# A four-layer forward and backward pass: the order of the weight-gradient products, the layout of dq, and which tiles are turned by DMA

## The chip, the cores and the metric

The kernel runs on one core of one Trainium2 chip. The metric is the device time of one execution in microseconds, the median of three runs. Engines: PE (TensorE, matrix products and 128x128 transposes), DVE (VectorE), ACT (ScalarE), POOL (GpSimd), and SP (SyncE), which here issues the DMA transfers, in the order of its own queue. PSUM, which PE writes, has eight banks.

## The reference

The forward pass runs four residual layers over x of 2048 x 640: linear attention (A), sliding-window attention (B), A, B, with one set of weights for both A and one for both B. 32 heads of 20 columns; the window of B is 256 tokens.

```python
def _A_ref(x, wqkv, wo):
    q, k, v = split(x @ wqkv)
    pq, pk = phi(q), phi(k)          # phi: t + 1 above 0, exp(t) below, + 1e-6
    kv, z = einsum("bhsd,bhse->bhde", pk, v), einsum("bhsd->bhd", pk)
    o = einsum("bhqd,bhde->bhqe", pq, kv) / (einsum("bhqd,bhd->bhq", pq, z)[..., None] + 1e-6)
    return merge(o) @ wo

def _B_ref(x, wqkv, wo):
    q, k, v = split(x @ wqkv)
    p = softmax(where(mask, q @ k.T * Dh ** -0.5, -1e9))   # 0 <= i - j < 256
    return merge(p @ v) @ wo

x = x + _A_ref(_layernorm(x), A_wqkv, A_wo)
x = x + _B_ref(_layernorm(x), B_wqkv, B_wo)
x = x + _A_ref(_layernorm(x), A_wqkv, A_wo)
x = x + _B_ref(_layernorm(x), B_wqkv, B_wo)
```

The outputs are the last x and the gradients of a given grad_out with respect to x and to the four weight matrices. Each weight gradient is a product over all tokens of two layers: for W, normed inputs (hn) transposed times the gradient of q, k, v (dq in DRAM, dqkv); for Wo, attention outputs (o) transposed times the layer's upstream gradient (gs).

## The kernel before

Tokens are cut into 16 tiles of 128, columns of 640 into five blocks of 128. The order of the instructions on each engine is written out by hand: each stage makes a list of (slot, function), sorts it, and runs it slot by slot. The table `PLACES` holds the slots. `put` queues a transfer for SP a few ticks later (delays in `PLACES["sp"]`), or issues it at once in the two linear stages, where SP's order is left to the framework. The stages of `passes`, in order of time:

- `forward`: layers 0 to 3. `plan_feat` makes the linear features of a tile; its `flip_h` turns hn2 into h2T on PE. `plan_front` of layer 2 needs the same turned tile again later to make the queries (`query`): it loads hn back from DRAM with a DMA transpose, as h3T. 
- `core` for layer 3, then for layer 1. A core walks over 8 chunks of two token tiles. Each chunk after the first has 24 visits, the first has 16, so that visits 24 to 47 are the second chunk (chunk 1). In `core_visit`, the visit that has just begun makes its scores s (PE), e = exp(s) (ACT) and the masks (POOL); the visit begun three steps earlier makes dp (PE) and ds = dp * e (DVE); ds is turned either on PE, with a copy out of PSUM by ACT or DVE (`flip_ds`, in which some extra warm transposes of the identity may stand), or by a DMA transpose, which `by_dma` says; the visit begun six steps earlier is multiplied into PSUM banks (`core_acc`). Every third visit `core_acc` adds the sums into the tile dq, [128, 2, 1920]: two token tiles by q, k and v columns. dp and s have one buffer each.
- `plan_behind` follows a core by about two chunks: dq is turned (`turn`), stored (`store`), multiplied by the turned weights WTB (`dh`), normalised backward (`ln`, `ln2`), multiplied by WoTA (`prod`) and summed into an outer product (`outer`). After the core its remainder, called left3 or left1, runs by itself.
- `plan_linear` does the backward pass of a linear layer, eight slots for each token tile: layer 2 between the two cores, layer 0 at the end.
- `weight_jobs` is a generator of all weight gradients. A job is one block of columns of one matrix (240 of W or 160 of Wo; twice that once `W.wide` is set). It keeps all rows of two layers in SBUF as lhs (2 x 16 tiles x 640) and the column block of 32 token tiles as rhs, and makes for each of the five row blocks m one PSUM sum over 32 products, copies it out (wr) and stores it. At m = 1 the next job's rhs is fetched, at m = 2, when the next job is of another matrix, its lhs. `W.lhs` lists the buffers that lhs take in turn; with `W.tight` the second lhs is fetched only after the job.
- `fill(us)` runs as many products of the generator as its credit of nominal time (columns / 2400 us for each product) allows. It is called in left1 with 0.7 us a slot from slot 25 on, in layer 0's stage with 0.8 us a slot, and with no bound afterwards. `W.tight` and `W.wide` change after layer 0's stage.

Before, the matrices come in the order B's Wo, B's W, A's Wo, A's W. `first` fetches the operands of the first job all at once at slot 3 of left1. PSUM during left1: two banks of the core's pool that are idle, four in a pool of its own, two for the weight jobs.

Of the kernel before, what the change touches and what calls it, by code (L numbers as in the profile page):

```python
# [11 lines left out]
ALU = mybir.AluOpType  # L12
# [3 lines left out]
P = 128  # L16
D = 640
# [31 lines left out]
    ld=[39.8, 61, 63, 69.7, 82.8],  # L49
    sp=[2.6, 1.1, -2.9, -3.4, 0.6, -3.8, 0.1, 0.4, 2, 1.8, 1.1, 0.8, 3, 1, 0.9, 0.5, 1.3, 1.1, 1, 1],  # L50
    ms=[1, -0.2, 20, 31.2, 39.5],
# [18 lines left out]
    xx=[1, 0, 1, 1, 0, 0, 0, 0, 1, 0, 1, 0, 0, 0, 0, 0, 0, 1, 0, 0, 1, 0, 0, 1],  # L70
    bd=[0, 1, 0, 0, 0, 0, 0, 1, 0, 1, 1, 0, 1, 1, 0, 0, 0, 1, 1, 1, 0, 1, 0, 0],
    sd=[0.7, 0, 0, 3, 3, 3, 3, 3.9, 0, 0, 3.2, 2.6, 3.3, 3.1],
    dj=[3, 21.9, 24, 3.5, 0.7, 8])

# [17 lines left out]
class Kern:  # L92
    def __init__(self, ctx, tc, x0, A_w, A_wo, B_w, B_wo, grad, outs):
        self.ctx, self.tc = ctx, tc
        self.nc = nc = tc.nc
        self.W = dict(A=A_w, B=B_w)
        self.Wo = dict(A=A_wo, B=B_wo)
        self.grad = grad
        self.out_x4, self.out_gx, dWA, dWoA, dWB, dWoB = outs
        self.dW = dict(A=dWA, B=dWB)  # L100
        self.dWo = dict(A=dWoA, B=dWoB)
        self.serial = 0
        self.queue, self.now, self.spm = [], 0, True
# [10 lines left out]
        self.x2 = d("x2", [T, D])  # L114
        self.WT = {k: d(f"WT{k}t", [P, NF * D]) for k in "AB"}
# [406 lines left out]
    def plan_front(self, st, la, lb, t, x, x_in, Wo, W, Wq=None):  # L522
# [6 lines left out]
        def load():  # L529
# [3 lines left out]
            else:  # L533
                x["h2T"] = st.fb.tile([P, DT, P], BF, name="h3T", bufs=2)
                self.dma(x["h2T"], self.rows(self.hn[la], t), transpose=True)

# [136 lines left out]
    def plan_feat(self, st, l, t, x, src, W):  # L673
# [5 lines left out]
        def flip_h():  # L679
            x["h2T"] = self.flip(st.ps, st.fl, x["hn2"], "h2T", P, DT, P, nc.scalar)  # L680

        def feat_(nm, c, split=False):
# [72 lines left out]
    @staticmethod  # L755
    def by_dma(n):

        return n >= 48 and PLACES["bd"][n % 24] == 1

# [91 lines left out]
    def core_acc(self, st, l, u):  # L851
# [28 lines left out]
        if u.last:  # L880
# [4 lines left out]

            def cols(tl, w, n):
                return tl[:, :, w * D:(w + n) * D].rearrange("p b (w q g x) -> p b w q g x", w=n, q=4, g=2)[:, :, :, u.qr, :, 40 * u.p:40 * u.p + 40]

            def acc(bk):
                return bk[:, 0:320].rearrange("p (b w g x) -> p b w g x", b=2, w=2, g=2)  # L890
            n = G * u.c + k
            if t0 + 2 < TT:
                nc.scalar.copy(st.part[:, n % (G + 1), :], st.acc[1][:, 0:320])
            else:
                for b in range(2):
                    nc.scalar.copy(cols(cur, 1, 2)[:, b], acc(st.acc[1])[:, b])  # L896
            if old is not None:
                for b in range(2):
                    nc.vector.tensor_tensor(out=cols(old, 1, 2)[:, b], in0=acc(st.acc[0])[:, b],
                                            in1=acc(st.part[:, (n + 1) % (G + 1), :])[:, b], op=ALU.add)  # L900
            nc.scalar.mul(cols(cur, 0, 1)[:, :, 0], st.acc[0][:, 320:480].rearrange("p (b g x) -> p b g x", b=2, g=2), CS)

# [64 lines left out]
    def plan_behind(self, st, l, c, dq, g_out):  # L967
# [16 lines left out]
        def turn(i):  # L984
            assert dq["n", c] == 8
            x["dT", i] = st.sp.tile([P, NF, P], BF, name="dqT", bufs=3)
            if c == TT // 2 - 2 or (c == TT // 2 - 1 and i == 0):
                self.turn_pe(st, x["dT", i], dq[c][:, i, :])
            else:
                self.put(7, x["dT", i], dq[c][:, i, :], transpose=True, delay=wait(0) if last else None)  # L990

        def store():
            assert dq["n", c] == 8
            self.put(8, self.pair(self.dq[l], c), dq.pop(c), delay=wait(tail))

# [25 lines left out]
        for i in range(2):  # L1021
# [3 lines left out]
            def dh(k, ci, i=i, t=t):  # L1025
# [9 lines left out]
                for kk in range(k, k + 5):  # L1035
                    self.mm(ps[:, 0:CW], x["dT", i][:, kk, :], st.WTB[:, kk, ci * CW:(ci + 1) * CW], kk == 0, kk == NF - 1)
                if k + 5 == NF:
# [209 lines left out]
    def weight_jobs(self, W):  # L1247
# [28 lines left out]

        def first(L, R, w):

            ls = [W.lhs.pop(0).tile([P, TT, D], BF, name="lhs") for _ in range(2)]
            r = operand()  # L1280
# [5 lines left out]
            return ls, r  # L1286
        mats = []
        for kind, layers, names in (("B", (3, 1), ("Wo", "W")), ("A", (2, 0), ("Wo", "W"))):
            for mat in names:
# [4 lines left out]
        def after(i, c0, w):  # L1294
# [5 lines left out]
            return i, c0, mats[i][3] * (2 if W.wide and c0 + 2 * mats[i][3] <= mats[i][4] else 1)  # L1300
        job, nxt = (0, 0, mats[0][3]), None
        while job is not None:
            i0, c0, w = job
            L, R, out = mats[i0][:3]
            if nxt is None:
                nxt = first(L, R, w)
                yield 0.0
            ls, r = nxt
            for m in range(DT):
# [7 lines left out]
                ps = W.ps.tile([P, 512], F32, name="wg")  # L1317
                for i in range(n):
                    self.mm(ps[:, 0:w], ls[i // TT][:, i % TT, m * P:(m + 1) * P], r[:, i, 0:w], i == 0, i == n - 1)
                    if i < n - 1:  # L1320
                        yield w / 2400.0
# [82 lines left out]
    def core(self, st, l, g_out, B, hooks):  # L1404
# [28 lines left out]
        with ExitStack() as es:  # L1433
            st.pS = self.pool(es, "pS", 1, bass.MemoryType.PSUM, "right")
            st.hist = []
            for c in range(NC):
                for qr in range(4):
                    S = B.slabs.pop(0)
                    for i, u in enumerate(self.core_visits(st, l, S, c, qr, dq)):
# [12 lines left out]
                        if n == (24 * c or self.V0) + st.lag:  # L1452
                            dq[c] = dqp.tile([P, 2, QT], BF, name="dq")
                        self.core_visit(st, l, u, slots[n], on_act[n], thin[n])
# [18 lines left out]
    def passes(self):  # L1473
# [6 lines left out]
        with ExitStack() as rest:  # L1480
# [92 lines left out]
            psl = ExitStack()  # L1573
            st.ps = self.psum(psl, "pl", 4)
            W.ps = self.pool(rest, "wp", 2, bass.MemoryType.PSUM, "right")
# [16 lines left out]
            for j, f in enumerate(left1):  # L1592
                if f is not None:
                    f()
                if j == min(int(PLACES["dj"][0]), len(left1) - 2):
                    next(jobs)
                if j == min(int(PLACES["dj"][1]), len(left1) - 1):
# [4 lines left out]
            self.close_outer(self.dmz)  # L1602
            self.turn_outer(st, self.dmz, self.dmzT)
            self.flush()
            psl.close()
# [3 lines left out]
            with ExitStack() as es, ExitStack() as le:  # L1609
# [4 lines left out]
                wl3 = self.pool(rest, "wl", 1)  # L1614
                W.lhs += [wl3, wl]
                lp = self.linear_pools(es, "right", 4)
# [4 lines left out]
                for f in self.slots(plan, int(max(a for a, *_ in plan)) + 1):  # L1621
                    if f is not None:
                        f()
                    fill(0.8)
            wl4 = self.pool(rest, "wl", 2)
            W.lhs += [wl4, wl4, wl2, wl3]
            W.tight, W.wide = False, True
# [70 lines left out]
```

## Time and profile before

| what | value |
|---|---|
| median of 3 runs | 2145.72 us (2145.54 to 2147.37) |
| profiled execution | 2146.71 us, its span 2145.0 us |
| granted PE clock, mean | 0.983 |
| DVE, ds, L812 | x368, 441.1 us |
| PE, weight-gradient products (wg) | x2880, 371.6 us |
| PE, turns of ds, L834 | x1920, 151.9 us |
| DMA transposes of ds | x120, 3.8 us to landing |
| DMA transposes into h3T | x16, 3.4 us to landing |

Order of the stages in the span: forward to about 650 us, core of layer 3 and its remainder to 1120, layer 2's linear stage to 1230, core of layer 1 to 1641, left1 to 1700, layer 0's stage with weight jobs to 1930, weight jobs alone to 2142.

How to read it: busy time is time in which an engine executed an instruction. A matmul's listed duration holds its latency; in a row of matmuls the distance between starts is shorter. PEld are weight loads, which lie beside PE's products. In lists of waits the name behind the arrow is what came last before the waiting instruction could start. A DMA share of 1 means that the core's 16 DMA engines had, on average, a packet under way all the time.

### The profile page before, as it was taken

How to read it: one execution, taken by the hardware profiler on the slowest of the kernel's cores; microseconds unless marked ns; L12 is line 12 of the kernel's file. 1: busy time of each engine (PE TensorE's matmuls, PEld its weight loads, DVE VectorE, ACT ScalarE, POOL GpSimd, SP SyncE). 2: the span in 40 equal slices, each digit the busy share in tenths (PEclk: the TensorE clock that was granted, in tenths of full speed). 3: DMA queues.
4: the chain of work that ended last, by engine and by line, in shares of the span. 5: the costliest groups of instructions: out<-in, count | busy, mean ns of one | idle time of the engine just before them, and what ended most of it. 6: DMA issues, size and time to landing. Idle time of an engine off the chain costs nothing.

```text
span 2145.0 us, 76508 instructions
## 1 busy us (share of the span) xinstructions
PE 2009.7 (94%) x32692; PEld 1555.7 (73%) x32692; DVE 1398.7 (65%) x2817; ACT 1310.1 (61%) x1846; POOL 1014.0 (47%) x1594
## 2 busy tenths in 40 slices
PE   9989998899988999999989999999998889999999
PEld 6667776677766877777768778777776878888644
DVE  7788886788856888888748778888885233320000
ACT  6558888478886787777637677777775143330000
POOL 1046666156665577777524456777764212220000
PEclk9999999999999999999989999999999999999999
DMA  7597876699984478898889734989889999989550
GB/s 252 200 229 209 211 208 174 194 229 213 226 201 137 134 158 190 185 193 174 177 274 260 211 91 121 187 190 187 187 175 210 273 299 253 261 203 283 190 166 21
DMA packets 659510, 425.42 MB, mean 198 GB/s; under 512 B 399328, under 2 KB 629472, under 8 KB 658912
## 3 DMA queue, kind: packets, MB, share of 16 engines
q1 hardware_dynamic: 659168, 420.52, 77.4%
q8 instruction: 255, 4.18, 0.8%
q14 instruction: 87, 0.71, 0.1%
HBM read 195.17 MB, written 144.70 MB: 158 GB/s over the span
## 4 chain that ended last, share of the span: by engine, by line
PE 52%; DVE 7%; ACT 6%; DMA 6%; issue 4%; POOL 3%; SPq 2%; DVEq 0%; ACTq 0%; POOLq 0%
PE dense L203 18%; PE wg L203 15%; DVE ds L812 5%; PE acc L203 4%; PE dp L203 3%; DMA pqb<-pqk 3%; PE flip L224 2%; PE flip L834 2%; ACT e L808 2%; SPq L147 2%; PE sT L203 1%; ACT eT L468 1%; PE ops L203 1%; ACT dsT L839 1%; PE flip L235 1%
## 5 line engine op out<-in xcount | busy, mean ns | idle before, releaser
L812 DVE TENSOR_TENSOR ds<-dp,e 128x1024 bf16<-128x1024 f32 (+1 forms) x368 | 441.1, 1199 | 109.4 <-PE s L203 68.0
L808 ACT ACTIVATE e<-s 128x1024 bf16<-128x1024 f32 (+1 forms) x368 | 372.4, 1012 | 114.1 <-PE s L203 97.1
L468 ACT ACTIVATE eT<-sT 128x2048 bf16<-128x2048 f32 x180 | 338.3, 1879 | 93.7 <-PE sT L203 78.5
L203 PE MATMUL wg<-rhs,lhs 128*128 128x240 bf16 (+3 forms) x2880 | 371.6, 285 | 5.9 <-DMA lhs<-o 5.9
L203 PEld LDWEIGHTS <-lhs 128*128 128x128 bf16 x2880 | 261.0, 98 | 93.5 <-DMA lhs<-o 6.6
L827 POOL TENSOR_SCALAR_AFFINE_SELECT e<-e 128x256 bf16<-128x256 bf16 x448 | 182.6, 422 | 138.3 <-ACT e L808 137.0
L203 PEld LDWEIGHTS <-dqT 128*128 128x128 bf16 x1920 | 174.0, 98 | 61.1 <-issue 5.0
L476 POOL TENSOR_SCALAR_AFFINE_SELECT eT<-eT 128x512 bf16<-128x512 bf16 x256 | 164.2, 645 | 112.9 <-ACT eT L468 108.9
L823 POOL TENSOR_SCALAR_AFFINE_SELECT e<-e 128x512 bf16<-128x512 bf16 x256 | 162.8, 636 | 85.5 <-ACT e L808 83.0
L203 PE MATMUL acc<-slabqs,ds 128*128 128x20 bf16 x2880 | 193.8, 172 | 2.1 <-ACT dq L896 0.4
L203 PE MATMUL acc<-ds,e 128*128 128x20 bf16 x2880 | 191.3, 171 | 0.0
L203 PEld LDWEIGHTS <-ds 128*128 128x128 bf16 x2880 | 172.3, 96 | 19.5 <-issue 15.1
L203 PE MATMUL dp<-slabT,dT 32*128 32x128 bf16 (+1 forms) x1920 | 148.2, 246 | 30.1 <-DVE ds L812 25.5
L1326 DVE CAST wr<-wg 128x240 bf16<-128x240 f32 (+3 forms) x54 | 24.4, 452 | 222.8 <-PE wg L203 216.7
L203 PEld LDWEIGHTS <-e 128*128 128x128 bf16 x2880 | 163.7, 96 | 4.9 <-issue 0.9
L203 PE MATMUL dense<-WB,hnT 128*128 128x320 bf16 x960 | 160.5, 301 | 1.2 <-ACT hnT L227 0.7
L1217 POOL TENSOR_TENSOR dh<-dh,lg 128x640 f32<-128x640 f32 x31 | 44.6, 1439 | 245.7 <-DVE s L1214 217.5
L1324 ACT CAST wr<-wg 128x240 bf16<-128x240 f32 (+3 forms) x36 | 14.3, 397 | 236.5 <-PE wg L203 234.1
L203 PE MATMUL dense<-WTA,dqT 128*128 128x320 bf16 x960 | 156.8, 300 | 1.2 <-DMA dqT<-dqa 0.6
L834 PE MATMUL flip<-ident,ds 128*128 128x128 bf16 x1920 | 151.9, 222 | 3.5 <-DVE ds L933 3.4
L203 PE MATMUL dense<-WTB,dqT 128*128 128x320 bf16 x960 | 153.8, 301 | 0.0
L479 POOL TENSOR_SCALAR_AFFINE_SELECT eT<-eT 128x512 bf16<-128x512 bf16 x224 | 143.9, 642 | 14.9 <-ACT eT L468 13.5
(187 smaller groups left out, 4440.0 us busy)
## 6 DMA issues: line engine op xcount, KB each, us to landing
T<-T SPq DMA_DIRECT2D x96, 256.0 KB, 3.8
s<-s SPq DMA_DIRECT2D x32, 512.0 KB, 3.2
slabT<-T SPq DMA_DIRECT2D x64, 256.0 KB, 3.7
dqkv<-dq SPq DMA_DIRECT2D x16, 960.0 KB, 6.6
dqkv<-dqa SPq DMA_DIRECT2D x32, 480.0 KB, 4.3
rhs<-dqkv SPq DMA_DIRECT2D x32, 480.0 KB, 6.1
rhs<-dqkv SPq DMA_DIRECT2D x16, 960.0 KB, 6.7
hn<-hn SPq DMA_DIRECT2D x64, 160.0 KB, 3.3
```

The lines of the kernel that those rows point to most:

```text
L147: return self.nc.sync.dma_start(out=out, in_=in_, transpose=transpose)
L203: return self.nc.tensor.matmul(out, lhsT=lhsT, rhs=rhs, start=start, stop=stop, skip_group_check=True, **kw)
L224: self.nc.tensor.transpose(t[0:w, j, :], src[:, c0:c0 + w], self.ident)
L468: nc.scalar.activation(e, s, ACT.Exp)
L476: nc.gpsimd.affine_select(out=e, in_=e, compare_op=ALU.is_ge, fill=0.0, base=0, pattern=[[0, 4], [1, P]], channel_multiplier=-1)
L479: nc.gpsimd.affine_select(out=e, in_=e, compare_op=ALU.is_ge, fill=0.0, base=-1, pattern=[[0, 4], [-1, P]], channel_multiplier=1)
L808: nc.scalar.activation(u.e[:, :, 0:w], s[:, :, 0:w], ACT.Exp)
L812: nc.vector.tensor_tensor(out=d.ds[:, :, 0:w], in0=d.dp[:, :, 0:w], in1=d.e[:, :, 0:w], op=ALU.mult)
L823: nc.gpsimd.affine_select(out=v, in_=v, pattern=[[0, 4], [1 if far else -1, P]], **kw)
L827: nc.gpsimd.affine_select(out=v, in_=v, pattern=[[0, 2], [1 if far else -1, P]], **kw)
L834: nc.tensor.transpose(ps[:, 4 * j + i, :], f.ds[:, j, i * P:(i + 1) * P], self.ident)
L1217: eng.tensor_tensor(out=x["dh"], in0=x["dh"], in1=L["g"][:, i, :], op=ALU.add)
```

## The change

Five edits.

1. `by_dma`: visits 24 to 47 of each core get a pattern of their own: every third visit, 8 of 24, is turned by DMA instead of PE. From visit 48 on the pattern is the old one.
2. `flip_h` of layer 2 also stores its turned tile in a DRAM array hT (put kind 20, delay 1.5), and `plan_front` of layer 2 loads h3T from there with a plain DMA.
3. dq is [128, 3840] with the columns in the order q0, k0, v0, k1, v1, q1, so that the k and v columns of both token tiles are one block. `core_acc` adds them in one instruction instead of two. The second token tile is turned in the order k, v, q; `dh` takes WTB's rows in that order; `store` writes three transfers instead of one.
4. The weight jobs begin with B's W. Its first column block is a lead job: five row blocks at once in three PSUM banks, over the token tiles in order, five products for each tile. Its operands are fetched in two halves, layer 3's at slot 3 of left1 and layer 1's at slot 12; at slot 16 the second job's rhs is fetched. The rest of the lead job is run before left1 ends. The banks come from left1's own pool, which keeps one; dense products and turns of left1 take that one and the core's two in turn.
5. The order of the matrices is B's W, B's Wo, A's Wo, A's W; the lhs buffers follow in another order; layer 0's stage fills 0.64 us a slot instead of 0.8. A second lhs that is missing when `W.wide` is set is fetched at once.

```diff
-    bd=[0, 1, 0, 0, 0, 0, 0, 1, 0, 1, 1, 0, 1, 1, 0, 0, 0, 1, 1, 1, 0, 1, 0, 0],
+    bd=[0, 1, 0, 0, 1, 0, 0, 1, 0, 0, 1, 0, 0, 1, 0, 0, 1, 0, 0, 1, 0, 0, 1, 0, 0, 1, 0, 0, 0, 0, 0, 1, 0, 1, 1, 0, 1, 1, 0, 0, 0, 1, 1, 1, 0, 1, 0, 0],
-    dj=[3, 21.9, 24, 3.5, 0.7, 8])
+    dj=[3, 21.9, 24, 3.5, 0.7, 8, 0.64, 12, 16])
...
-                self.dma(x["h2T"], self.rows(self.hn[la], t), transpose=True)
+                self.dma(x["h2T"].rearrange("p a q -> p (a q)"), self.hT[t])
...
             x["h2T"] = self.flip(st.ps, st.fl, x["hn2"], "h2T", P, DT, P, nc.scalar)
+            if l == 2:
+                self.put(20, self.hT[t], x["h2T"].rearrange("p a q -> p (a q)"))
...
-        return n >= 48 and PLACES["bd"][n % 24] == 1
+        return PLACES["bd"][24 + n % 24 if n >= 48 else n - 24] == 1 if n >= 24 else False
...
             if old is not None:
-                for b in range(2):
-                    nc.vector.tensor_tensor(out=cols(old, 1, 2)[:, b], in0=acc(st.acc[0])[:, b],
-                                            in1=acc(st.part[:, (n + 1) % (G + 1), :])[:, b], op=ALU.add)
+                nc.vector.tensor_tensor(out=cols(old)[:, 1:5], in0=acc(st.acc[0]), in1=acc(st.part[:, (n + 1) % (G + 1), :]), op=ALU.add)
...
-            self.put(8, self.pair(self.dq[l], c), dq.pop(c), delay=wait(tail))
+            src, to = dq.pop(c), self.pair(self.dq[l], c)
+            self.put(8, to[:, 0], src[:, 0:QT], delay=wait(tail))
+            self.put(8, to[:, 1, D:QT], src[:, QT:QT + 2 * D], delay=wait(tail))
+            self.put(8, to[:, 1, 0:D], src[:, QT + 2 * D:2 * QT], delay=wait(tail))
...
-        for kind, layers, names in (("B", (3, 1), ("Wo", "W")), ("A", (2, 0), ("Wo", "W"))):
+        for kind, layers, names in (("B", (3, 1), ("W", "Wo")), ("A", (2, 0), ("Wo", "W"))):
...
+        for _ in first(ls, r, L, R, w):
+            yield 0.0
+        job = after(0, 0, w)
+        nxt = ls, rhs(R, job[1], job[2])
+        yield 0.0
+        banks = [W.lead.tile([P, 512], F32, name="wg") for _ in range((DT + 1) // 2)]
+        begun = [None] * len(banks)
+        for i in range(n):
+            for m in range(DT):
+                b = m // 2
+                ins = self.mm(banks[b][:, m % 2 * w:(m % 2 + 1) * w], ls[i // TT][:, i % TT, m * P:(m + 1) * P], r[:, i, 0:w],
+                              begun[b] is None, i == n - 1)
...
+                yield w / 2400.0
...
+        W.led = True
...
                 for i in range(n):
+                    if W.wide and nxt[0][1] is None:
+                        nxt[0][1] = lhs(L2[1])
...
-            st.ps = self.psum(psl, "pl", 4)
+            W.led, W.lead = False, self.psum(psl, "wf", 3)
+            st.ps = Turns((self.psum(psl, "pl", 1), st.ps2, st.ps2))
...
-                if j == min(int(PLACES["dj"][0]), len(left1) - 2):
-                    next(jobs)
+                for a in (0, 7, 8):
+                    if j == min(int(PLACES["dj"][a]), len(left1) - 2):
+                        next(jobs)
...
+            while not W.led:
+                next(jobs)
...
-                W.lhs += [wl3, wl]
+                W.lhs += [wl3]
...
-                    fill(0.8)
+                    fill(PLACES["dj"][6])
...
-            W.lhs += [wl4, wl4, wl2, wl3]
+            W.lhs += [wl4, wl4, wl2, wl, wl3]
```

More of the change, by code (lines that the diff above doesn't have):

```diff
@@ L49 @@
     ld=[39.8, 61, 63, 69.7, 82.8],
-    sp=[2.6, 1.1, -2.9, -3.4, 0.6, -3.8, 0.1, 0.4, 2, 1.8, 1.1, 0.8, 3, 1, 0.9, 0.5, 1.3, 1.1, 1, 1],
+    sp=[2.6, 1.1, -2.9, -3.4, 0.6, -3.8, 0.1, 0.4, 2, 1.8, 1.1, 0.8, 3, 1, 0.9, 0.5, 1.3, 1.1, 1, 1, 1.5],
     ms=[1, -0.2, 20, 31.2, 39.5],
@@ L114, in __init__ @@
         self.x2 = d("x2", [T, D])
+        self.hT = d("hT", [TT, P, D])
         self.WT = {k: d(f"WT{k}t", [P, NF * D]) for k in "AB"}
@@ L884, in core_acc, with cols @@
             k = 2 * u.qr + u.p
-            def cols(tl, w, n):
-                return tl[:, :, w * D:(w + n) * D].rearrange("p b (w q g x) -> p b w q g x", w=n, q=4, g=2)[:, :, :, u.qr, :, 40 * u.p:40 * u.p + 40]
+            def cols(tl):
+                return tl.rearrange("p (a q g x) -> p a q g x", a=6, q=4, g=2)[:, :, u.qr, :, 40 * u.p:40 * u.p + 40]
             def acc(bk):
-                return bk[:, 0:320].rearrange("p (b w g x) -> p b w g x", b=2, w=2, g=2)
+                return bk[:, 0:320].rearrange("p (a g x) -> p a g x", a=4, g=2)
             n = G * u.c + k
@@ L894, in core_acc @@
             else:
-                for b in range(2):
-                    nc.scalar.copy(cols(cur, 1, 2)[:, b], acc(st.acc[1])[:, b])
+                nc.scalar.copy(cols(cur)[:, 1:5], acc(st.acc[1]))
             if old is not None:
-                for b in range(2):
-                    nc.vector.tensor_tensor(out=cols(old, 1, 2)[:, b], in0=acc(st.acc[0])[:, b],
-                                            in1=acc(st.part[:, (n + 1) % (G + 1), :])[:, b], op=ALU.add)
-            nc.scalar.mul(cols(cur, 0, 1)[:, :, 0], st.acc[0][:, 320:480].rearrange("p (b g x) -> p b g x", b=2, g=2), CS)
+                nc.vector.tensor_tensor(out=cols(old)[:, 1:5], in0=acc(st.acc[0]), in1=acc(st.part[:, (n + 1) % (G + 1), :]), op=ALU.add)
+            nc.scalar.mul(cols(cur)[:, 0:6:5], st.acc[0][:, 320:480].rearrange("p (b g x) -> p b g x", b=2, g=2), CS)
     def slots(self, plan, n):
@@ L987, in turn @@
             if c == TT // 2 - 2 or (c == TT // 2 - 1 and i == 0):
-                self.turn_pe(st, x["dT", i], dq[c][:, i, :])
+                self.turn_pe(st, x["dT", i], dq[c][:, i * QT:(i + 1) * QT])
             else:
-                self.put(7, x["dT", i], dq[c][:, i, :], transpose=True, delay=wait(0) if last else None)
+                self.put(7, x["dT", i], dq[c][:, i * QT:(i + 1) * QT], transpose=True, delay=wait(0) if last else None)
         def store():
             assert dq["n", c] == 8
-            self.put(8, self.pair(self.dq[l], c), dq.pop(c), delay=wait(tail))
+            src, to = dq.pop(c), self.pair(self.dq[l], c)
+            self.put(8, to[:, 0], src[:, 0:QT], delay=wait(tail))
+            self.put(8, to[:, 1, D:QT], src[:, QT:QT + 2 * D], delay=wait(tail))
+            self.put(8, to[:, 1, 0:D], src[:, QT + 2 * D:2 * QT], delay=wait(tail))
         def load_o():
@@ L1035, in dh @@
                 for kk in range(k, k + 5):
-                    self.mm(ps[:, 0:CW], x["dT", i][:, kk, :], st.WTB[:, kk, ci * CW:(ci + 1) * CW], kk == 0, kk == NF - 1)
+                    self.mm(ps[:, 0:CW], x["dT", i][:, kk, :], st.WTB[:, (kk + DT * i) % NF, ci * CW:(ci + 1) * CW], kk == 0, kk == NF - 1)
                 if k + 5 == NF:
@@ L1275, in rhs, with first @@
             return t
-        def first(L, R, w):
-            ls = [W.lhs.pop(0).tile([P, TT, D], BF, name="lhs") for _ in range(2)]
-            r = operand()
+        def first(ls, r, L, R, w):
             for i in range(2):
@@ L1285, in first @@
                         self.dma(ls[i][:, b:b + E, :], L[i][b * P:(b + E) * P, :].rearrange("(t p) f -> p t f", p=P))
-            return ls, r
+                yield
         mats = []
-        for kind, layers, names in (("B", (3, 1), ("Wo", "W")), ("A", (2, 0), ("Wo", "W"))):
+        for kind, layers, names in (("B", (3, 1), ("W", "Wo")), ("A", (2, 0), ("Wo", "W"))):
             for mat in names:
@@ L1300, in after @@
             return i, c0, mats[i][3] * (2 if W.wide and c0 + 2 * mats[i][3] <= mats[i][4] else 1)
-        job, nxt = (0, 0, mats[0][3]), None
+        L, R, out, w = mats[0][:4]
+        ls = [W.lhs.pop(0).tile([P, TT, D], BF, name="lhs") for _ in range(2)]
+        r = operand()
+        for _ in first(ls, r, L, R, w):
[10 more added lines that the diff above has]
+                              begun[b] is None, i == n - 1)
+                if begun[b] is None:
+                    begun[b] = ins
+                else:
+                    self.after(ins, begun[b])
+                yield w / 2400.0
+        for m in range(DT):
+            o = W.out()
+            src = banks[m // 2][:, m % 2 * w:(m % 2 + 1) * w]
+            if m % 2:
+                nc.scalar.copy(o[:, 0:w], src)
+            else:
+                nc.vector.tensor_copy(o[:, 0:w], src)
+            self.put(0, out[m * P:(m + 1) * P, 0:w], o[:, 0:w], delay=PLACES["dj"][3])
+        W.led = True
         while job is not None:
@@ L1304, in weight_jobs @@
             L, R, out = mats[i0][:3]
-            if nxt is None:
-                nxt = first(L, R, w)
-                yield 0.0
             ls, r = nxt
@@ L1452, in core @@
                         if n == (24 * c or self.V0) + st.lag:
-                            dq[c] = dqp.tile([P, 2, QT], BF, name="dq")
+                            dq[c] = dqp.tile([P, 2 * QT], BF, name="dq")
                         self.core_visit(st, l, u, slots[n], on_act[n], thin[n])
```

## The prediction

> **What bounds the kernel now.** I read the page first, then busy time by stretch, then the chain that ended last, then the instructions in order of time around the gaps, then the issues of SP's queue. The page says TensorE (PE) is the engine with the most work:
>
> ```profile
> PE 2009.7 (94%) x32692; PEld 1555.7 (73%) x32692; DVE 1398.7 (65%) x2817; ACT 1310.1 (61%) x1846; POOL 1014.0 (47%) x1594
> ```
>
> The part that the change rebuilds begins at 1640 us, after layer 1's core. The stretches (columns: PE, PEld, DVE, ACT, POOL busy, granted clock, DMA share, GB/s) show where PE does not work there:
>
> ```profile
> 1655.00:1660.00 5.00, 1.98 (x15) 1.18 (x15) 1.45 (x4) 2.11 (x4) 3.98 (x3) 1.00 0.99 275
> 1670.00:1680.00 10.00, 4.14 (x44) 3.19 (x42) 1.95 (x5) 2.13 (x4) 4.47 (x3) 0.82 1.12 383
> 1680.00:1690.00 10.00, 10.00 (x109) 9.08 (x108) 2.88 (x7) 0.98 (x2) 2.37 (x3) 0.84 1.00 302
> 1745.00:1755.00 10.00, 4.45 (x54) 3.73 (x53) 3.01 (x8) 4.20 (x9) 2.93 (x2) 0.83 1.06 374
> 1755.00:1760.00 5.00, 5.00 (x35) 3.73 (x34) 1.19 (x3) 0.85 (x2) 0.00 (x0) 0.66 0.70 261
> 1780.00:1930.00 150.00, 149.36 (x1543) 132.09 (x1541) 45.19 (x121) 53.17 (x112) 34.00 (x23) 1.00 1.02 240
> ```
>
> Outside three gaps PE is full. The chain of waits names the last two, and PE's instructions in order of time show the first of these two:
>
> ```profile
> 1669.21 9.61 DMA lhs<-o
> ...
> 1734.06 10.49 DMA lhs<-hn
> 1744.96 9.19 DMA ldn<-dn
> ```
>
> ```profile
> 1675.58 0.45 PE L203 MATMUL wg<-rhs,lhs 128*128 128x160 bf16 x4 [2.56 <-DMA lhs<-o]
> 1678.86 0.72 PE L203 MATMUL wg<-rhs,lhs 128*128 128x160 bf16 x4 [2.83 <-DMA lhs<-o]
> ```
>
> Gap A (1670 to 1680, 5.86 us idle): the first weight-gradient job runs row block 0 over all 32 token tiles, so after 28 short products it needs the last lhs piece; these loads were issued from 1653.95 to 1670.9, slowed by full DMA. Gap B (1745 to 1755, 5.55 us idle): B's change from Wo to W puts 16 transfers in front of layer 0's loads of dn, and PE's next flip waits. The 3.02 us at 1655 wait for POOL's gn and are not touched.
>
> **What the tail gains.** PE's total does not change: 12 products of 160 columns take 0.83 us on the chain and 8 of 240 columns 0.82, that is 4.32 and 4.27 ns per 10 columns, so width buys nothing. Only gaps and granted clock count.
>
> Gap A: the lead job needs five products for each token tile, so its 16 first tiles last 80 x 0.1025 = 8.2 us. Its first half (3.5 MB) is issued at slot 3 (1654), at the stretch's 335 GB/s landed by about 1665; the second by about 1676. Filling starts at 1670.25, tile 16 is due after 1678. So both 2.5 to 2.8 us waits go. The granted clock was 0.64 in 1675 to 1680 and 0.67 in 1680 to 1685; with 1.59 and 5.00 us of PE work there, 1.59 x 0.36 + 5.00 x 0.33 = 2.2 us goes too. Late next is POOL's gn of the last tile, ready at 1675.4 while its flip would come near 1674.5: 1.0 us stays. Net -5.86 - 2.2 + 1.0 = **-7.0** (bounds -8.1 and 0).
>
> The Trainium skill (TensorE: Matmul & The Clock Gate, HAM oscillation — how this bites in real kernels) lets the clock fall after idle gaps of over about 3.4 us; here two gaps of 2.56 and 2.83 us with 0.45 us of work between them brought it to 0.64, so the trace is harsher than that rule read gap by gap. By the rule the 2.2 us would not have been lost to this gap and the forecast would be 2.2 us later; I go by the row.
>
> Gap B: B's W runs first and lasts through layer 0's loop, so no lhs change falls into it: the idle 5.55 us and the slow clock in 1750 to 1760 (0.80 x 0.35 + 5.00 x 0.34 = 2.0 us) go. **-7.5** (bounds -7.5 and 0).
>
> Given back. Credits: 22 slots x 0.7 = 15.4 us pay 154 of the lead's 160 products; the loop's 158 slots x 0.64 = 101 us pay 1011 of the 1120 left in W. So the loop ends inside W's last job, about 108 products (11 us) before Wo. Wo's first lhs has a free buffer (wl3) and can come early, as one lhs<-hn came at 1843, long before its use. Its second goes into wl4, laid where layer 0's pools were: if free 5 us after the loop, 2.56 MB at the 360 GB/s of 1960 to 1970 plus 2 us of latency land 14 us after the loop, 2 to 3 us late. I take **+3.0** (0 if it comes early; 15 if all 6.4 MB wait for the loop: 5 + 18 us against 11, and some 3 us of clock). In before the same kind of change at 1972 cost 0.5 us. Layer 0's first flips come sooner in a shorter slot (5.0 us from load to flip at 1704.6, 4.4 us is the landing): **+0.5** (0 to 4). Left1 has three PSUM banks in turn instead of four; layer 1's core ran its dense products on two: **+0.5** (0 to 3). Evictions of the lead's five blocks (3 x 0.41 on DVE, 2 x 0.36 on ACT) lie beside PE. WTA's load, last in SP's order, moves some 7 us later, to land near 1693; its first product was at 1723.6. Tail: -7.0 - 7.5 + 4.0 = **-10.5**.
>
> **Layer 0's loop.** A tile took 12.61 us, 8 slots, all PE. At 0.64 instead of 0.8 it is 8 x 0.16 x 1.025 = 1.31 us less, 11.30; that work moves behind the loop and costs nothing unless DMA cannot follow. A pair of tiles moves 3.2 MB of its own and the rhs take 0.64 x 8 / 16 x 1.92 = 0.61 MB a tile, transposes 0.48: 2.7 MB in 11.30 us, 240 GB/s, where 1830 to 1900 ran 268 GB/s without one PE wait. Nothing is added; the other case is a rival.
>
> **The cores.** Chunk 1 of each core turns its ds on PE in all 24 visits, with five warm transposes each; 8 of them now go by DMA.
>
> ```profile
> 701.00:750.00 49.00, 47.50 (x1153) 40.97 (x1150) 43.86 (x58) 37.75 (x52) 29.13 (x58) 1.00 0.42 134
> 1273.00:1322.00 49.00, 47.43 (x1158) 41.14 (x1157) 43.59 (x59) 37.85 (x54) 29.53 (x58) 1.00 0.28 82
> L841 DVE COPY dsT<-flip 128x1024 bf16<-128x1024 bf16 x128 | 87.0, 679 | 0.0
> L899 DVE TENSOR_TENSOR dq<-acc,part 128x160 bf16<-128x160 f32 x224 | 61.4, 315 | 5.2 <-PE acc L203 4.9
> L203 PE MATMUL dense<-WA,h3T 128*128 128x320 bf16 x160 | 26.6, 299 | 2.3 <-DMA h3T<-hn 0.9 <-DVE r L559 0.9 <-DVE s L589 0.3
> ```
>
> PE is full there, DMA is not. A visit without its 13 transposes spares PE 0.45 + 0.35 = 0.8 us and DVE a 0.68 us copy. But dp, ds and the next dp share one buffer: the starts of ds, eight visits at a time, never average under 1.98 us in the later chunks before the drain, and chunk 1's 24 starts (700.74 to 750.36) take 49.6 us, 2.07 each. So at most 24 x 0.09 = 2.1 us a core; I take half and a little, 1.2, both cores **-2.4**. Against it: a DMA turn takes SP 1.23 us and lands in 3.8 us (median); its use is three visits (6 us) later. The worst PE wait on one was 1.1 us; 16 of those is +18 on the other side.
>
> dq's sums become one DVE instruction of 320 elements instead of a pair of 0.55 us; the nearest row of that size (a 320-column product out of PSUM, 0.49) saves 0.06 x 112 = 6.7 us of DVE. DVE holds 7% of the chain against 65% busy, so a ninth counts: **-0.7** (-6.7 to 0). Three stores of dq for one are 32 more SP issues of about 0.42 us; what stands behind them is the next slab load or dqT turn, and SP waits for engines meanwhile, so I take 0 (up to +2).
>
> The saved h2T: 16 loads take the place of 16 DMA transposes of 1.21 us on SP, against 16 stores of 160 KB in layers 1 and 2's forward, where PE was 49.8 of 50 us busy and DMA 0.82. PE and its weight loads waited 2.9 us for h3T, and the T turns behind it on SP another 2: **-1.5** (-5 to +1).
>
> Sum: -10.5 - 2.4 - 0.7 - 1.5 = -15.1 on the profiled execution's 2146.7 (span 2145.0 and 1.7 around it): 2131.6. That run lies 1.0 above the median of 2145.7, so about **2131**.
>
> **Rivals.** (1) The stalls move to the new operand changes, Wo and then A's Wo, since one W job's last blocks are too short for 5.1 MB: +10 to +12 on the forecast, **2142**. For it: gaps A and B are of this kind. Against: SP had loads up to 100 us early when the buffer was free. (2) Slower: layer 0's loop becomes DMA's. Its share is 1.02 to 1.2 already, and layer 2's same stage took
>
> ```profile
> 1170.41 2.50 PE dense L203 x25
> ...
> 1183.88 2.63 PE dense L203 x29
> ```
>
> 13.4 us a tile at 283 GB/s. At that interval 12 tiles lose 12 x 2.05 = 24.6 us, **2155**; it decides from 12.5 us a tile on, where the gain is used up. Against: the bytes above, and layer 2's DVE is 85% busy where layer 0's is 33%. (3) The lead waits anyway, for gn or its banks, and the core's edits are hidden: only gap B and h2T remain, -7.5 - 1.5 + 4, **2140**.
>
> **Chances.** Forecast 0.54, own range 2122 to 2139; (1) 0.18; (2) 0.14; (3) 0.14. A difference counts from 0.2%, 4.3 us, that is under 2141.4 or over 2150.0. Faster: 0.54 + 0.08 + 0.12 = 0.74; within: 0.10 + 0.02 + 0.01 = 0.13; slower, all of (2) beyond 2150 and a rest, 0.13. The range takes the low bounds of dq, h2T and the cores together at half (-10) and on the high side (1) with its clock: 2119 to 2149.
>
> **What would show it.** Right: no PE wait for lhs or ldn between 1660 and 1770, clock 1.00 there; a tile interval of 11.3 us; the loop over near 1890; ds starts of 2.0 us in chunk 1. Wrong: a wait of over 5 us for lhs<-o after the loop (1), PE idle and dqT waits in the loop (2), lead products waiting (3), or waits of acc for dsT in chunk 1.

## The result, and the profile after

The changed kernel takes 2129.57 us in the median of ten runs against 2146.71 us of the kernel before, a ratio of 0.9924 with a 95% interval of 0.991 to 0.9939. Single runs of one kernel lie further apart than the gain (before: 2135.6 to 2157.6 in one set of 30), so what follows is read from stretches inside the profiled executions as well as from ratios. Its profiled execution took 2126.94 us, span 2125.2. The page's first part:

```profile
PE 1987.4 (94%) x32332; PEld 1530.7 (72%) x32332; DVE 1388.1 (65%) x2696; ACT 1300.8 (61%) x1818; POOL 1014.0 (48%) x1594
```

The stretches where before had its gaps A and B, and layer 0's loop (columns as before: PE, PEld, DVE, ACT, POOL busy, granted clock, DMA share, GB/s):

```profile
1670.00:1680.00 10.00, 10.00 (x97) 9.07 (x95) 2.37 (x5) 0.69 (x1) 4.17 (x4) 1.00 1.17 319
1680.00:1690.00 10.00, 9.53 (x100) 8.77 (x98) 3.06 (x7) 1.32 (x3) 0.00 (x0) 1.00 0.82 293
1690.00:1700.00 10.00, 8.47 (x92) 7.76 (x90) 1.73 (x5) 1.95 (x3) 0.00 (x0) 1.00 0.90 275
1700.00:1745.00 45.00, 45.00 (x518) 40.47 (x516) 18.62 (x45) 20.89 (x42) 7.04 (x5) 1.00 0.80 238
1745.00:1760.00 15.00, 15.00 (x168) 13.58 (x167) 7.79 (x17) 5.39 (x11) 4.71 (x4) 1.00 1.01 261
1760.00:1890.00 130.00, 129.96 (x1352) 113.70 (x1350) 42.53 (x114) 50.53 (x106) 33.54 (x22) 1.00 1.02 252
1890.00:1900.00 10.00, 10.00 (x99) 9.39 (x97) 1.77 (x5) 1.90 (x4) 2.94 (x2) 1.00 0.36 108
1900.00:1910.00 10.00, 9.01 (x114) 8.64 (x112) 0.73 (x2) 0.65 (x2) 0.00 (x0) 1.00 0.88 290
```

PE is full from 1700 to 1900, the clock stays at 1.00, and none of these stretches idles more than 1.53 us. What PE still waits for at the two places that change, in its instructions in order of time, is small (ldn and lpqk are layer 0's loads of dn and of its features):

```profile
1698.60 0.55 PE L225 MATMUL flip<-ident,lpqk 128*120 128x128 bf16 x6 [1.25 <-DMA lpqk<-pqk]
...
1906.73 5.43 PE L204 MATMUL wg<-rhs,lhs 128*128 128x160 bf16 x76 [0.99 <-DMA lhs<-o]
```

The second line is W's change to Wo behind the loop. SP's queue shows why it costs 1 us. Here are one transfer of the first lhs at 1840, inside the loop (the first of them was at 1805), and the second lhs as soon as layer 0's pools are free:

```profile
1840.64 0.49 SPq L148 DMA_DIRECT2D lhs<-o  x1
1896.49 2.40 SPq L148 DMA_DIRECT2D lhs<-o  x4
```

The chain of waits gives the loop's pace, one such piece in each tile:

```profile
1809.31 1.23 PE wg L204 x12
...
1820.59 1.33 PE wg L204 x13
...
1831.87 1.33 PE wg L204 x13
```

That is 11.28 us a tile against 12.61 before. The group of dq's sums (out<-in, count | busy, mean ns | idle before):

```profile
L900 DVE TENSOR_TENSOR dq<-acc,part 128x320 bf16<-128x320 f32 x112 | 54.2, 484 | 5.7 <-PE acc L204 5.7
```

54.2 us instead of 61.4.

**Where the 19.8 us between the two profiled spans lie.** Marks: the first and last ds of each core (its starts on DVE).

| stretch | before | after | difference |
|---|---|---|---|
| start to first ds of layer 3's core | 669.33 | 668.01 | -1.3 |
| layer 3's core to its last ds | 398.41 | 396.03 | -2.4 |
| to the first ds of layer 1's core | 173.28 | 168.94 | -4.3 |
| layer 1's core to its last ds | 395.02 | 394.85 | -0.2 |
| last ds to the end (the tail) | 508.96 | 497.37 | -11.6 |

One pair of profiles cannot tell which of these belong to the change; the runs below do.

### The profile page after: what moved, and what is told of

The parts are those of the page before. It is cut to its first block, busy times and chain, and to the rows that moved or that the text cites. A ratio compares the mean times of both kernels' runs of the same rounds, so it can differ in the third digit from the quotient of the medians.

```text
span 2125.2 us, 75617 instructions
## 1 busy us (share of the span) xinstructions
PE 1987.4 (94%) x32332; PEld 1530.7 (72%) x32332; DVE 1388.1 (65%) x2696; ACT 1300.8 (61%) x1818; POOL 1014.0 (48%) x1594
## 4 chain that ended last, share of the span: by engine, by line
PE 53%; DVE 8%; ACT 6%; DMA 4%; issue 4%; POOL 4%; SPq 1%; DVEq 0%; POOLq 0%; ACTq 0%
PE dense L204 19%; PE wg L204 15%; DVE ds L815 5%; PE acc L204 5%; PE dp L204 3%; PE flip L225 2%; PE flip L837 2%; DMA pqb<-pqk 2%; ACT e L811 2%; PE sT L204 1%; ACT eT L469 1%; PE ops L204 1%; POOL e L830 1%; POOL e L826 1%; ACT dsT L842 1%
## 5 line engine op out<-in xcount | busy, mean ns | idle before, releaser
L204 PEld LDWEIGHTS <-lhs 128*128 128x128 bf16 x2720 | 250.8, 98 | 93.6 <-DMA lhs<-o 1.2
L204 PE MATMUL s<-slabT,slabqT 32*128 32x128 bf16 (+1 forms) x1920 | 146.6, 248 | 4.2 <-DMA slabqT<-T 1.7
```

The lines of the kernel that those rows point to most:

```text
L204: return self.nc.tensor.matmul(out, lhsT=lhsT, rhs=rhs, start=start, stop=stop, skip_group_check=True, **kw)
```

## The experiments

My theory after the result: the tail is the weight jobs' work, chunk 1 of the cores the DMA turns', and the other stretches are chance. Rivals: the core's edits carry half; the lead job or the order alone is enough; the loop's fill does not matter.

A profile shows one execution. Those of lead_only, fill8 and dve_thin1 are the longest of the twelve of each kernel: they show where time goes, and the ratios, from all twelve, show how much it is.

### The parts by themselves

**jobs_alone** and **core_alone** take the change apart: one has only edits 4 and 5, the other only 1 to 3. In short, each is the changed kernel with the lines of the other edits put back:

```diff
# jobs_alone
-        return PLACES["bd"][24 + n % 24 if n >= 48 else n - 24] == 1 if n >= 24 else False
+        return n >= 48 and PLACES["bd"][n % 24] == 1
...
-                self.dma(x["h2T"].rearrange("p a q -> p (a q)"), self.hT[t])
+                self.dma(x["h2T"], self.rows(self.hn[la], t), transpose=True)
...
# core_alone
-        for kind, layers, names in (("B", (3, 1), ("W", "Wo")), ("A", (2, 0), ("Wo", "W"))):
+        for kind, layers, names in (("B", (3, 1), ("Wo", "W")), ("A", (2, 0), ("Wo", "W"))):
...
-                    fill(PLACES["dj"][6])
+                    fill(0.8)
```

> The kernel before with the weight jobs of the change alone (lead job, order of the matrices, lhs buffers, fill of 0.64); the pattern of by_dma, hT and the layout of dq are those of before. Theory: the profile after lost 11.6 us behind the last ds of layer 1's core (509.0 to 497.4), and this part does that alone: ratio to before 0.9945 (11.6 of 2146.7), between 0.993 and 0.996; wg begins in left1 with no wait for lhs. Rival (the core's edits and luck carry half): ratio above 0.9965.

> The kernel before with by_dma's new visits, hT and the new layout of dq; the weight jobs are those of before. Theory: chunk 1 of each core gives 1.5 to 1.8 us, the rest nearly nothing, so -3 to -5 us: ratio 0.9975 to 0.9985, with both gaps of the tail as in before (about 5.5 us each). Rival: the 4.3 us that the profile after is shorter between the last ds of layer 3's core and the first of layer 1's come from dq's layout and stores, so -8 us: ratio 0.9963.

Measured: jobs_alone 0.993 (0.9905 to 0.9956), its tail 2136.2 - 1639.68 = 496.5 us; core_alone 0.9992 (0.9976 to 1.0008), its tail 511.3. The weight jobs carry the tail, the core's edits none of it. core_alone lies above the range that its theory gave (0.9975 to 0.9985), and its interval takes in no gain at all. The stretch between the cores took 168.8 and 168.6 us in these two and 168.3 to 170.7 in the two below; three of the four have before's code there, so before's 173.3 was chance. So was the start: the first ds of layer 3's core came between 667.4 and 676.6 us in fourteen profiles whose forward pass differs, if at all, in hT.

**order_only** and **lead_only** take the weight jobs apart.

```diff
# order_only, from the kernel before
-        for kind, layers, names in (("B", (3, 1), ("Wo", "W")), ("A", (2, 0), ("Wo", "W"))):
+        for kind, layers, names in (("B", (3, 1), ("W", "Wo")), ("A", (2, 0), ("Wo", "W"))):
...
-                    fill(0.8)
+                    fill(0.64)
...
# lead_only, from jobs_alone
-        for kind, layers, names in (("B", (3, 1), ("W", "Wo")), ("A", (2, 0), ("Wo", "W"))):
+        for kind, layers, names in (("B", (3, 1), ("Wo", "W")), ("A", (2, 0), ("Wo", "W"))):
...
-    dj=[3, 21.9, 24, 3.5, 0.7, 8, 0.64, 12, 16])
+    dj=[3, 21.9, 24, 3.5, 0.7, 8, 0.8, 12, 16])
...
```

> The kernel before with the other order alone: B's W first, its operands fetched all at once, the first job row block by row block; lhs buffers and fill of 0.64 as in the change. Theory: gap A stays, near 1670 (products wait for the last lhs piece, 4 to 7 us with the clock at 0.65 behind it); gap B is gone; the loop's tile interval is 11.3 us; ratio 0.997 to 0.998. Rival (the order does not matter without the lead, because the stall only moves behind the loop): ratio 0.999 or more, with over 5 us of wait for lhs<-o after the loop.

> The kernel before with the lead job alone: five row blocks as operands land, fetched in two halves, but of B's Wo (160 columns), and with the order, the lhs buffers and the fill of 0.8 of before. Theory (the waits for lhs in left1 end through the five products per landed tile, gap B is another matter): left1 gains about 7 us, but with 160 columns the lead has consumed its first half after 16 x 5 x 0.069 = 5.5 us instead of 8.2, so up to 2 us of wait may stay; gap B stays at 5 us; ratio 0.9965 to 0.998. Rival (one cause, DMA full in this stretch, and only W first relieves it): gap A stays above 4 us, ratio 0.9985 to 1.0.

order_only: 0.9968 (0.9951 to 0.9986), tail 506.2, 2.8 us less than before. The stretches at gap A and at the start of layer 0:

```profile
1670.00:1680.00 10.00, 7.57 (x48) 5.79 (x49) 1.45 (x3) 0.69 (x1) 0.68 (x1) 0.66 1.04 404
1695.00:1705.00 10.00, 6.39 (x65) 5.86 (x64) 0.41 (x1) 0.36 (x1) 0.00 (x0) 1.00 0.68 222
```

Gap A stayed, with four waits for lhs of 4.3 us in all and the clock at 0.66. The second gap is not one that I expected. PE's wait and SP's queue just before it:

```profile
1704.24 0.56 PE L224 MATMUL flip<-ident,ldn 128*126 128x128 bf16 x6 [3.61 <-DMA ldn<-dn]
...
1689.54 7.89 SPq L147 DMA_DIRECT2D out_dram<-wr  x3
1697.52 0.39 SPq L147 DMA_DIRECT2D rhs<-dqkv  x1
1698.00 0.53 SPq L147 DMA_DIRECT2D ldn<-dn  x1
```

SP stands 7.9 us in three stores that wait for row blocks PE has yet to finish, and layer 0's first load is behind them. The lead job ends all five blocks before left1 does; there the first ldn was on time.

lead_only: 1.0012 (0.9995 to 1.003), tail 511.0: against the theory. Gap A was closed (no wait for lhs in left1), but PE lost more further on:

```profile
1706.72 1.23 PE L203 MATMUL wg<-rhs,lhs 128*128 128x160 bf16 x8 [8.92 <-DVE wr L1352]
...
1689.14 9.57 SPq L147 DMA_DIRECT2D rhs<-in_grad_out_dram  x2
1698.81 3.88 SPq L147 DMA_DIRECT2D rhs<-g  x2
1702.78 2.85 SPq L147 DMA_DIRECT2D out_dram<-wr  x5
```

A lead of 160 columns ends before left1 does, so a second job starts inside left1. Its rhs fetch for the third job goes into the lead's buffer and waits on SP for PE's products (8.6 us in all), the lead's five stores stand behind it, and all five buffers wr are taken. **lead_wr10** doubles these buffers and changes nothing else:

```diff
-            wo = self.pool(rest, "wo", 5)
+            wo = self.pool(rest, "wo", 10)
```

> The lead job of Wo in the kernel before, with ten buffers wr instead of five. In the run with five, PE waited 8.9 us for a copy into wr: the lead's five blocks held all five buffers, and on SP their stores stood behind the third job's rhs, which waits for the lead's own rhs buffer. Theory: that wait goes (at most 1 us left), gap A stays closed, gap B stays at 4 to 5 us; from the last ds of layer 1's core to the end 501 to 504 us (511.0 with five, 509.0 before). Rival (PE would have waited for SP's jam anyway): 508 us or more.

Measured: 0.9981 (0.9962 to 0.9999), tail 503.2; no wait for wr, gap B at its old place with 5.4 us:

```profile
1674.00:1684.00 10.00, 10.00 (x135) 9.43 (x133) 2.91 (x6) 0.69 (x1) 4.20 (x5) 1.00 1.12 325
1740.00:1750.00 10.00, 4.63 (x39) 3.67 (x37) 1.65 (x5) 2.38 (x6) 1.96 (x2) 0.85 1.06 379
```

So the lead alone is worth 5.8 us of tail (509.0 to 503.2) once its stores have room: that is gap A. These are single profiles; core_alone, whose tail has before's code, came out 2.3 us over before. The 5.8 of the lead and the 2.8 of the order make 8.6, and the change's own tail is 11.6 shorter: the rest of the gain needs both.

**fill8** puts the change of matrix back inside layer 0's loop:

```diff
-    dj=[3, 21.9, 24, 3.5, 0.7, 8, 0.64, 12, 16])
+    dj=[3, 21.9, 24, 3.5, 0.7, 8, 0.8, 12, 16])
...
-                W.lhs += [wl3]
+                W.lhs += [wl3, wl]
...
-            W.lhs += [wl4, wl4, wl2, wl, wl3]
+            W.lhs += [wl4, wl4, wl2, wl3]
```

> The changed kernel with a fill of 0.8 us instead of 0.64 in layer 0's stage and the lhs lists of before behind it, so that B's W ends inside the stage and Wo's lhs are loaded there. Theory (an lhs change inside layer 0's loop is what made gap B): a wait of 4 to 9 us for lhs<-o or for layer 0's own loads near 1850, with the clock down behind it; from the last ds of layer 1's core to the end 502 to 507 us instead of 497.4. Rival (gap B came from the queue at the start of the stage, not from the change of matrix): no such wait, 496 to 499 us.

Measured: 0.9958 (0.9935 to 0.998), tail 504.2. The chain of waits and SP's queue at the place:

```profile
1909.56 8.00 DMA dqT<-dqa
1917.61 1.51 PE dense L204 x5
```

```profile
1904.98 0.37 SPq L148 DMA_DIRECT2D lhs<-o  x1
1906.33 0.35 SPq L148 DMA_DIRECT2D out_dram<-wr  x1
1906.73 1.66 SPq L148 DMA_DIRECT2D lhs<-o  x3
1909.08 0.38 SPq L148 DMA_DIRECT2D out_dram<-lgn  x1
1909.56 4.25 SPq L148 DMA_TRANSPOSE dqT<-dqa  x2
```

This time the turns of dqa (layer 0's gradient of q, k and v), not the loads of dn, stood behind four transfers of 640 KB, and PE waited 8.1 us, at the loop's end and not near 1850. The mechanism of gap B is shown: an lhs change inside the loop puts bulk in front of what the loop needs next. It takes transfers in a row: the changed kernel's first lhs, also loaded inside the loop but two transfers at 1805 and one at 1840, cost no wait.

### The cores

**no_warm** undoes the DMA turns and takes the five warm transposes of each chunk 1 visit away instead; **dve_thin1** takes them away beside the DMA turns (and has the last chunks' elementwise work on DVE, see below).

```diff
# no_warm: by_dma as before, and
-    WARM = (8, 5)
+    WARM = (8, 0)
# dve_thin1: by_dma as changed, and the same line
```

> The changed kernel, but chunk 1 of both cores turns all ds on PE again (by_dma as before) and has no warm transposes (WARM 8 and 0 instead of 8 and 5). Theory: a chunk cannot go under 1.98 us a visit because dp and ds share one buffer, and any 0.35 us of PE freed per visit gets most of the way: 24 starts of ds in 47.8 to 48.6 us, clock 1.00, ratio as the changed kernel's (0.9924 +- 0.0015). Rival (the warm transposes hold the granted clock up): clock under 0.95 in chunk 1 and more than 50 us for it.

> The changed kernel with the last two chunks' elementwise work on DVE and, in chunk 1, no warm transposes beside the 8 DMA turns. Theory (1.98 us a visit is a floor set by dp's and ds's one buffer, and 8 DMA turns have already reached it but for 0.3 us): chunk 1 in 47.5 to 48.3 us, no gain over 0.5 us a core; tail 493 to 495 us; ratio about 0.991. Rival (PE is still the limit in the 16 visits that PE turns): chunk 1 under 47.3 us.

| chunk 1, 24 starts of ds | layer 3, us | granted clock | layer 1, us | granted clock |
|---|---|---|---|---|
| no DMA turns (before, jobs_alone, order_only, lead_only, lead_wr10) | 49.45 to 49.62 | 1.00 | 49.78 to 49.81 | 1.00 |
| 8 DMA turns (the change and six runs that keep it) | 47.79 to 50.12, mean 48.96 | 0.90 to 1.00 | 48.06 to 49.06, mean 48.38 | 0.93 to 0.96 |
| no_warm | 49.11 | 0.97 | 48.27 | 0.96 |
| dve_thin1 | 50.04 | 0.80 | 51.22 | 0.73 |

The DMA turns cost some of the clock, which the prediction did not have. Where nothing goes by DMA and all warm transposes stand, the clock of chunk 1 was 1.00 in all ten stretches; in the fourteen with the change's pattern it was 1.00 in one, and on the whole the chunk is longer the lower the clock: 47.79 us at 1.00, 48.06 to 48.29 at 0.96, 48.56 to 49.37 at 0.93, 50.12 at 0.90.

no_warm's ratio is 0.992 (0.9895 to 0.9945), like the changed kernel's, and its chunk 1 is near the means of the row above it: as far as this can tell, freeing 0.35 us of PE in each visit is worth as much as freeing 0.8 us in every third. Its theory had the clock at 1.00 and both chunks under 48.6 us; the clock and layer 3's chunk missed that, and its rival's clock under 0.95 did not come either. dve_thin1 (0.9947, 0.9929 to 0.9965) has the slowest chunk 1 in layer 1, and in layer 3 only fill8's is slower, against both theories. Its stretches say why:

```profile
707.00:757.00 50.00, 42.51 (x991) 35.36 (x989) 41.41 (x49) 35.07 (x50) 29.66 (x59) 0.80 0.67 159
1279.00:1330.00 51.00, 43.93 (x989) 36.44 (x987) 41.21 (x49) 34.92 (x50) 29.48 (x59) 0.73 0.57 108
```

The granted clock was 0.80 and 0.73. The same stretches of the changed kernel, with 69 and 78 more PE instructions, had more of it:

```profile
699.00:747.00 48.00, 41.10 (x1069) 35.48 (x1063) 41.91 (x48) 34.88 (x50) 29.77 (x60) 1.00 0.67 169
1264.00:1312.00 48.00, 41.64 (x1058) 36.05 (x1055) 41.78 (x48) 34.48 (x49) 29.30 (x59) 0.96 0.54 118
```

It is not this one execution: over all of the kernel, dve_thin1's twelve runs had a mean clock of 0.971 to 0.981, the six of after_again beside them 0.982 to 0.988. So the change stands where taking more work from PE costs clock.

**no_dq** puts dq's old layout back, **after_again** repeats the changed kernel beside it.

```diff
# no_dq
-                nc.vector.tensor_tensor(out=cols(old)[:, 1:5], in0=acc(st.acc[0]), in1=acc(st.part[:, (n + 1) % (G + 1), :]), op=ALU.add)
+                for b in range(2):
+                    nc.vector.tensor_tensor(out=cols(old, 1, 2)[:, b], in0=acc(st.acc[0])[:, b],
+                                            in1=acc(st.part[:, (n + 1) % (G + 1), :])[:, b], op=ALU.add)
...
```

> The changed kernel with dq in its old layout: two additions instead of one, one store instead of three. Theory (DVE's 0.07 us a pair are hidden under PE in five of six chunks, and SP has room for the stores): the same within what can be measured, ratio within 0.0015 of the changed kernel's; DVE loses about 8 us of idle time. Rival (DVE is on the path, as 7% of the chain says and more): 3 to 6 us slower.

> The changed kernel as it is, so that the other three of this set have it on the same chip: ratio 0.991 to 0.994, 497 us from the last ds of layer 1's core to the end.

0.993 (0.991 to 0.995) against 0.9928 (0.9905 to 0.995), tails 494.3 and 494.8: nothing that can be told from zero. As far as this shows, DVE's 7 us are hidden.

**dve_behind** aims at what PE still waits for in left1; **dve_no_th** takes away the other warm transposes.

```diff
# dve_behind
-            return nc.vector if last and PLACES["td"][6 * (l == 1) + 3 * i + k] else nc.gpsimd
+            return nc.vector if last and PLACES["td"][6 * (l == 1) + 3 * i + k] or l == 1 and c >= TT // 2 - 2 else nc.gpsimd
# dve_no_th: the same, and
-    th=[0, 2, 1, 4, 1, 0, 0, 0, 0, 3, 0, 1, 0, 0, 0, 4, 8, 5, 0, 1, 2, 2, 1, 1],
+    th=[0] * 24,
```

> The changed kernel with the last two chunks' elementwise work behind layer 1's core (dh + g, gn, the folds) on DVE instead of POOL. DVE is 29% busy in 1650 to 1700, PE still waits there some 4 us for POOL's gn and what follows it (1.40 and 1.54 us on POOL; the same 640 columns took DVE 0.81). Theory: 2 to 3 us less between the last ds and the end, 494.5 to 496 us, ratio about 0.991. Rival: DVE then holds up the core's last ds or the copies of dqT, and nothing is won or some is lost: 497 us or more.

> The changed kernel with the last two chunks' elementwise work on DVE, and without the 36 warm transposes that a chunk still has from visit 48 on (about 2.5 us of PE a chunk, 6 chunks, two cores). Theory (a visit there is PE's, 2.2 us on average against a floor of 1.98, so freed PE counts in part): a chunk of 24 visits falls from 52.9 us on average to 51 to 52.5, together 5 to 20 us less, ratio 0.983 to 0.990. Rival (they fill time in which PE would wait, or hold the clock): chunks stay at 52.5 to 53.5 us or the clock falls, ratio 0.990 or more.

dve_behind: 0.9918 (0.9889 to 0.9947), PE's waits for gn in the tail fall from 2.8 to 0.8 us, its tail is 493.8; but the two others with the same edit have 495.6 and 496.2, and five kernels with POOL have 494.3 to 497.4. No gain is shown. dve_no_th: 0.9924 (0.9903 to 0.9945). The visits after chunk 1 took 313.4 and 311.5 us of the two cores, against 317.0 and 315.6 in the profile after and 315.2 and 312.0 in after_again: 0.4 to 4.0 us a core less, which the ratio does not show. No version was found that beats the changed kernel by more than can be measured.

## Why the prediction came out

**The sum was right, 2131 for 2129.57, by its largest term, the tail, and in part by luck.** The tail gained about 3.5 us more than forecast; 2.2 us for dq and h2T and 0.5 us in chunk 1 did not come, and these errors nearly cancel.

- Gap A, -7.0: shown. Its waits are gone in all runs with the lead and there in order_only; from left1's first row of dense products (at 1646.63 before and 1639.54 after) to the turn of dmz (1699.60 and 1685.36) lie 52.97 and 45.82 us, 7.2 us less. lead_wr10 puts it at 5.8 by itself, from one profile on each side.
- Gap B, -7.5: gone, and its mechanism is shown by fill8, which brings a stall of 8.1 us back. But the step "B's W first, so no lhs change falls into the loop" left out a condition: order_only has no more lhs change in the loop than the changed kernel and still loses 3.6 us and some of the clock (0.66 from 1705 to 1710) on ldn, because stores of unfinished blocks stood in front of it on SP. The lead job clears these too.
- Given back, +4.0: mis-sized. W's change to Wo cost 1.0 us instead of 3.0 (0.6 to 2.0 in the other runs that keep it), since the first lhs came early, as one of the two cases had it, and the second within 10 us. Layer 0's first flips waited 1.2 us for lpqk instead of 0.5 for dn, and three banks cost nothing that shows. That is 2.2 us in place of 4.0.
- The tail: -10.5 forecast. The five profiles with all of edits 4 and 5 and POOL have 494.3 to 497.4, mean 496.0; before and core_alone 509.0 and 511.3, mean 510.1. That is -14. The pair of profiles has -11.6, and the terms as measured, -7.2 - 7.5 + 2.2, make -12.5; where the rest lies is not traced.
- The loop: 11.30 us a tile forecast, 11.28 measured, PE busy 129.96 of 130.00 us; rival 2 fell. The loop's last PE work was at 1890, as forecast. Rival 2's price was a misreading: its two lines of layer 2's stage, at 1170.41 and 1183.88, span two tiles, with the same piece of the first at 1177.27 between them. Layer 2 took 6.6 to 6.9 us a tile there, so its DMA rate spoke against the rival and not for it.
- Chunk 1, -2.4: means of 48.96 and 48.38 against 49.49 and 49.80 make -0.5 - 1.4 = -1.9. The floor of 1.98 us a visit (47.5 us) was not reached in the mean. The term counted the freed PE time and left out the clock, which fell from 1.00 to between 0.90 and 1.00. Whether the 1.9 us reach the end is not shown: core_alone's -1.7 us (0.9992) has an interval of -5.1 to +1.7.
- dq, -0.7, and h2T, -1.5: not found. Between the first and last product of h3T lie 208.2 us before and 208.1 after, and 208.1 to 208.7 in all fourteen profiles, with either way of loading. The waits for h3T that I priced were 2.9 us before and are 2.5 after: a plain load is waited for as a transpose was. What failed is the step from a wait in a list to time on the path.
- Rival 1 (stalls move to the new operand changes) fell: 0.99 us. Rival 3 (the lead waits anyway) fell for the changed kernel; lead_only shows that it was close, with another column count.

What stays open: why layer 3's chunk 1 gains less than layer 1's. The clock goes with the spread inside each layer, but its mean over the seven profiles is 0.95 in both.

## What to carry to other kernels

When a product accumulates over operands that are still arriving, order it so that each landed piece is used for all its products before the next is needed; but count the buffers in which its results leave at once, and what stands in front of their stores. On an in-order DMA queue, a transfer that waits for work not yet done (a store of an unfinished block, a load into a buffer in use) delays everything behind it, so place bulk operand changes where nothing latency-bound follows. Sizes of waits in a list are not gains: the two stalls of 5.9 and 5.6 us that idled PE whole and took the clock with them came back as time; 2.9 us for h3T, 2.0 us for gn and DVE's 7 us did not, as far as these runs can tell. And work taken from PE can cost clock: look at the granted clock beside the busy time.

## What the runs showed of the hardware

The granted clock does not fall after long gaps alone. In dve_thin1 PE was busy 85 to 86% of the time (42.51 of 50 us and 43.93 of 51) in many short pieces. Its list of waits for these stretches holds one group, 13 and 12 waits for ds of 7.5 and 7.1 us in all, the longest 0.8 us, and the clock fell to 0.80 and 0.73. In the changed kernel, with 7 to 8% more PE instructions there, it was 1.00 and 0.96, and 0.90 to 1.00 over seven profiles. Such a figure is a mean: from 1305 to 1328 dve_thin1 ran at 0.50. The share of busy time alone does not set it: 41.10 of 48 us (86%) went with 1.00, no_warm's 43.46 of 48 (91%) with 0.96, and a slower clock makes PE's own work longer (in before, five dense products took 1.54 us at 1679.37, where the clock was 0.50, and 0.84 us at 1684.77, where it was 1.00). What the hardware counts, these runs do not show.

Gap A in before, two waits of 2.56 and 2.83 us, went with a clock of 0.64 as well. The Trainium skill (TensorE: Matmul & The Clock Gate, HAM oscillation — how this bites in real kernels) names idle gaps of over about 3.4 us; these gaps were shorter. The Trainium skill's next section there (A second HAM failure mode) tells of a kernel in which frequent short idles between groups of matmuls made the clock swing: dve_thin1's stretches agree, with no wait over 0.8 us.
